# The projected queries' scratch laid out by part instead of by head

## The chip, the cores and the metric

The kernel runs on one core of a Trainium2 chip. The metric is the device time of one execution in microseconds (us); the median of several executions counts. A profile is taken of one further execution by the hardware's profiler. The engines are PE (TensorE, matrix products; PEld is its weight load), DVE (VectorE), ACT (ScalarE), POOL (GpSimd) and SP (SyncE, which here only issues transfers). Sixteen DMA engines move the data of the transfers.

## The reference

A gate mixes two branches of the same input x (2048 tokens of 512 values): attention with 32 query heads of 16 values that share one key and one value head, and a SwiGLU feed-forward of width 1792.

```python
def _A_ref(x, wq, wk, wv, wo):
    q = (x @ wq).reshape(B, S, H, Dh).transpose(0, 2, 1, 3)      # H = 32, Dh = 16
    k, v = x @ wk, x @ wv
    p = softmax(einsum("bhqd,bkd->bhqk", q, k) * Dh ** -0.5)
    o = einsum("bhqk,bkd->bhqd", p, v)
    return o.transpose(0, 2, 1, 3).reshape(B, S, H * Dh) @ wo

def _B_ref(x, w_gate, w_up, w_down):
    return (silu(x @ w_gate) * (x @ w_up)) @ w_down

g = sigmoid((x * gate_w).sum(-1, keepdims=True))
return g * _A_ref(x, ...) + (1 - g) * _B_ref(x, ...)
```

## The kernel before

**Numbers.** Everything is fp32. A product of full precision is made of three products of a faster format: each operand is split into a high part (rounded) and a low part (the rest), and high x high, high x low and low x high are added in PSUM. `load_split` (L135) does that for a weight: it loads a raw tile `wraw` (two buffers), and GpSimd writes the high part (L107) and the low part (L108).

**Queries.** `query(m, c)` (L214) projects 128 columns of the queries, which are 8 heads of 16 values, for 512 tokens: m and c each run from 0 to 3. Its `keep` leaves three parts, each 128 rows (8 heads x 16) by 512 tokens: `ql` (low), `qh` (high) and `qb`, the absolute value times the largest key, whose product with a row of -1 in the key tile is a bound that keeps the exponent safe without a maximum. `store` (L246) writes the three to a scratch in the chip's memory, `q_d`, 48 transfers of 256 KB in all. The four jobs of m = 0 run before the attention and put off their stores to `run(STORES, NCH)` (L650); the twelve others run among the first head's scores, until about 130 us. From m = 1 on, VectorE makes all three parts in buffers `hh`, `hl` (seven each) and `hs`, `ht` (two each), which are free again when their store has landed.

**Loads of a head.** `load_head(h)` (L660) brings one head's queries back. The tile `qs` (two buffers, so one head ahead) has 128 partitions: two halves of 64 rows, one for the even and one for the odd chunks of 512 tokens, and in each half the rows of high, low, high, bound. So each half needs the high part once by itself and then low, high and bound, which lie next to each other in the scratch. Head h+1 is loaded after the block in which head h starts.

**The main loop.** A unit is one head and 128 keys. `score` (L673) makes two matmuls for 1024 queries, one on each half of TensorE's rows at the same time (L680); ScalarE exponentiates (L688), on some tiles after VectorE's copy (L684); `mix` (L692) multiplies with the values (L700). The feed-forward's matmuls (L192) are put between, step by step, each job first on the lower and then on the upper half of the rows. Four units make a block. The order on each engine is written out by `block` and its tables inside `manual_schedule`; the first loads and stores before it are placed by the framework's scheduler.

**What stands in SP's queue.** Almost all transfers are issued by SP, in order: a transfer that waits for its data or its buffer holds up all behind it. Besides the stores and loads of `q_d` these are the weights (raw tiles for the first two of four passes over the feed-forward's weights, L138; the split parts are stored in the second pass, L160, and loaded in the third and fourth, L166) and a finished head's output (L714). Each transfer ends on one of eight semaphores, in turn; an instruction that needs it waits for that one.

**If the bound fails**, a plain softmax from L876 on computes everything again; with these inputs that part isn't run.

Of the kernel before, what the change touches and what calls it, by code (L numbers as in the profile page):

```python
# [8 lines left out]
F32 = mybir.dt.float32  # L9
# [9 lines left out]
P = 128  # L19
S = 2048  # L20
D = 512
H = 32
DH = 16
# [3 lines left out]
CH = 512  # L27
# [3 lines left out]
HG = P // DH  # L31
KR = 3 * DH
RT = 64
# [29 lines left out]
def tile_gated_mix(ctx, tc, x, wq, wk, wv, wo, w_gate, w_up, w_down, gate_w, out):  # L63
    nc = tc.nc
# [4 lines left out]
    dpool = ctx.enter_context(tc.tile_pool(name="dpool", bufs=1, space=DRAM))  # L69
# [1 line left out]
    ps_o = ctx.enter_context(tc.tile_pool(name="ps_o", bufs=1, space=PSUM))  # L71
    ps_f = ctx.enter_context(tc.tile_pool(name="ps_f", bufs=3, space=PSUM))

    q_d = dpool.tile([H, 3 * DH, S], F32, name="q_d")
    o_d = dpool.tile([D, S], F32, name="o_d")
    a_d = dpool.tile([NCH, P, TC, D], F32, name="a_d")
    x_d = dpool.tile([2, 2, P, KD, CH], F32, name="x_d")
# [33 lines left out]
    def three(a, b, sa, sb):  # L111
        return [(a[0][sa], b[0][sb]), (a[0][sa], b[1][sb]), (a[1][sa], b[0][sb])]
# [101 lines left out]
    def query(m, c):  # L214
        cs = slice(c * CH, (c + 1) * CH)
        t = m * NCH + c

        def terms():
            r = []
            for k in range(KD):  # L220
                r += three(WQ[m], XC[c], (slice(None), k), (slice(None), k))
            return r

        def keep(ps):
            qh = wp.tile([P, CH], F32R, name="hh", bufs=7)
            ql = wp.tile([P, CH], F32R, name="hl", bufs=7)

            if m:
                qb = wp.tile([P, CH], F32, name="ht" if c % 2 else "hs", bufs=2)
                nc.vector.tensor_copy(qh, ps)  # L230
            else:
                qb = wp.tile([P, CH], F32R, name="hl" if c % 2 else "hh", bufs=7).bitcast(F32)
                nc.scalar.activation(qh, ps, AF.Copy)
                nc.scalar.activation(qb.bitcast(F32R), ps, AF.Abs, scale=kmax)
            nc.vector.tensor_tensor(ql, ps, qh.bitcast(F32), ALU.subtract)
            if m:
                nc.vector.tensor_scalar(qb, qh.bitcast(F32), kmax, None, op0=ALU.mult)
                nc.vector.scalar_tensor_tensor(qb.bitcast(F32R), qb, -1.0, qb, op0=ALU.mult, op1=ALU.max)
            parts = [ql, qh, qb.bitcast(F32R)]
            if not m:  # L240
                for h, qs in QS.items():
                    for i, part in enumerate([qh] + parts):
                        row = c % 2 * RT + i * DH
                        nc.sync.dma_start(qs[row:row + DH, c // 2, :].bitcast(F32), part[h * DH:(h + 1) * DH].bitcast(F32))

            def store():  # L246
                for j, part in enumerate(parts):
                    nc.sync.dma_start(q_d[m * HG:(m + 1) * HG, j * DH:(j + 1) * DH, cs], part.bitcast(F32))

            if m:  # L250
                store()
            else:
                STORES.append(store)
            nc.vector.tensor_reduce(top[:, t:t + 1], qb, axis=AX.X, op=ALU.max)

        return Job(3 * KD, lambda: m in WQ, terms, keep)
# [211 lines left out]
    def output(pool):  # L468
        w = []
        for k in range(KD):  # L470
            raw = pool.tile([P, D], F32, name="os", bufs=4)
            nc.sync.dma_start(raw, wo[k * P:(k + 1) * P, :])
            w.append([pool.tile([P, D], F32R, name=f"w{x}{k}", bufs=1) for x in "hl"])
            split(w[k][0], w[k][1], raw)
        for c in range(NCH):
            o = [pool.tile([P, KD, CH], F32R, name=n, bufs=1) for n in ("oh", "ol")]
            for k in range(KD):
                raw = pool.tile([P, CH], F32, name="os", bufs=4)
                nc.sync.dma_start(raw, o_d[k * P:(k + 1) * P, c * CH:(c + 1) * CH])
                split(o[0][:, k, :], o[1][:, k, :], raw)  # L480
            for i in range(TC):
                t = c * TC + i
                ps = ps_f.tile([P, CH], F32, name="pf")
                terms = []
                for k in range(KD):
                    terms += three([x[:, k] for x in o], w[k], (slice(None), slice(i * P, (i + 1) * P)), slice(None))
                mm(ps, terms)
                at = pool.tile([P, D], F32, name="at")
                nc.sync.dma_start(at, a_d[c, :, i, :])
                ot = pool.tile([P, D], F32, name="ot")  # L490
                nc.vector.scalar_tensor_tensor(ot, ps, g_sb[:, t:t + 1], at, op0=ALU.mult, op1=ALU.add)
                nc.sync.dma_start(out[t * P:(t + 1) * P, :], ot)
# [4 lines left out]
    def new_qs(h):  # L497
        QS[h] = qsp.tile([P, 2, CH], F32R, name="qs")
        return QS[h]
# [157 lines left out]
    with tc.tile_pool(name="bpool", bufs=2) as bp:  # L657
        PT = {}

        def load_head(h):  # L660
            qs = new_qs(h).bitcast(F32)
            qv = q_d[h].rearrange("r (j b s) -> b r j s", b=2, s=CH)
            for b in range(2):

                nc.sync.dma_start(qs[b * RT:b * RT + DH], qv[b, DH:2 * DH])
                nc.sync.dma_start(qs[b * RT + DH:(b + 1) * RT], qv[b])


        def new_pt(u):
# [61 lines left out]
        def block(k, first, last, steps, kinds, order):  # L731
# [51 lines left out]
            halves.clock += 2 * LONG  # L783

        load_head(1)
        for n in range(2):
            load_w("g", n)
# [3 lines left out]
        with tc.manual_schedule():  # L791
# [25 lines left out]
            for k in range(2 * BEGIN // BLOCK, NB):  # L817
# [8 lines left out]
                h = u // NT  # L826
# [49 lines left out]
    with tc.If(rv != 0):  # L876
        with tc.tile_pool(name="gpool", bufs=2) as gp:
            with tc.For_i(0, H, 1) as h:
                qg = gp.tile([KR, S], F32R, name="qg", bufs=1)
                nc.sync.dma_start(qg[0:DH, :].bitcast(F32), q_d[bass.ds(h, 1), DH:2 * DH, :])  # L880
                nc.sync.dma_start(qg[DH:, :].bitcast(F32), q_d[bass.ds(h, 1), 0:2 * DH, :])
                for qt in range(NT):
                    pr = gp.tile([P, S], F32, name="pr")
                    mx = gp.tile([P, 3], F32, name="mx")
                    halves = []
                    for half in range(2):
                        ps = ps_s.tile([P, 2 * CH], F32, name="pss")
                        for j in range(2):
                            c = half * 2 + j
                            nc.tensor.matmul(ps[:, j * CH:(j + 1) * CH], qg[:, qt * P:(qt + 1) * P],  # L890
                                             ks[:KR, c * CH:(c + 1) * CH], start=True, stop=True)
                        nc.vector.tensor_reduce(mx[:, half:half + 1], ps, axis=AX.X, op=ALU.max)
                        halves.append(ps)
                    nc.vector.tensor_tensor(mx[:, 2:3], mx[:, 0:1], mx[:, 1:2], ALU.max)
                    nc.vector.tensor_scalar(mx[:, 2:3], mx[:, 2:3], -SCALE, None, op0=ALU.mult)
                    for half in range(2):
                        nc.scalar.activation(pr[:, half * 2 * CH:(half + 1) * 2 * CH], halves[half], AF.Exp,
                                             scale=SCALE, bias=mx[:, 2:3])
                    po = ps_o.tile([P, CH], F32, name="po")
                    for b in range(NT // TC):  # L900
                        pt = ps_f.tile([P, CH], F32, name="pf")
                        for i in range(TC):
                            kt = b * TC + i
                            nc.tensor.transpose(pt[:, i * P:(i + 1) * P], pr[:, kt * P:(kt + 1) * P], ident)
                        ptc = gp.tile([P, CH], F32, name="ptc")
                        nc.vector.tensor_copy(ptc, pt)
                        for i in range(TC):
                            kt = b * TC + i
                            nc.tensor.matmul(po[:2 * DH, :P], vaug[:, kt, :], ptc[:, i * P:(i + 1) * P],
                                             start=(kt == 0), stop=(kt == NT - 1))  # L910
                    og = gp.tile([2 * DH, 2, P], F32, name="og")
                    nc.vector.tensor_copy(og[:, 0, :], po[:2 * DH, :P])
                    nc.vector.stream_shuffle(og[:, 1, :], og[:, 0, :], [DH] * 2 * DH)
                    nc.vector.reciprocal(og[:, 1, :], og[:, 1, :])
                    nc.vector.tensor_tensor(og[:, 0, :], og[:, 0, :], og[:, 1, :], ALU.mult)
                    nc.sync.dma_start(o_d[bass.ds(h * DH, DH), qt * P:(qt + 1) * P], og[:DH, 0, :])
        with tc.tile_pool(name="upool", bufs=2) as up:
            output(up)
# [31 lines left out]
```

## Time and profile before

| what | us |
|---|---|
| median of 3 executions (1341.17 to 1343.2) | 1342.19 |
| the profiled execution, its whole time | 1340.92 |
| its span, first to last instruction | 1339.1 |
| TensorE busy | 1327.4 (99%) |
| ScalarE busy | 1069.0 (80%) |
| VectorE busy | 710.3 (53%) |
| GpSimd busy | 220.3 (16%) |
| sixteen DMA engines, transfers issued by SP | 36.4% of their span |

The busy shares are averages. The "chain" of the profile follows the last instruction back to whatever released each step; a wait on it is time that the whole kernel took longer. The rows of SP are issues: they tell when and for how long SP was occupied with a transfer, not how long the data moved. The stores of the queries run from 44 to 130 us, the loads of the heads from 71 to 1198 us.

### The profile page before, as it was taken

Reading aid. Unit: us, or ns where it says so; the run is one execution under the profiler, and the core shown is the slowest. Engines: PE = TensorE matmul, PEld = TensorE weight load, DVE = VectorE, ACT = ScalarE, POOL = GpSimd, SP = SyncE. Lnnn points to the kernel's source line nnn. Section 1 sums busy time; section 2 is a strip of 40 time slices with the busy share of each in tenths; the row PEclk is TensorE's granted clock in tenths of the full one; section 3 lists DMA queues with packets and bytes.
Section 4 is the critical chain, followed back from the end, with each engine's and each line's share of the span. In section 5 each row is a group of like instructions: output and inputs, shape, how many; then the busy total and the mean of one; then the engine's idle time right before and its main releaser. Section 6 shows DMA issues by size and latency. Waiting matters only on the chain.

```text
span 1339.1 us, 26770 instructions
## 1 busy us (share of the span) xinstructions
PE 1327.4 (99%) x10743; PEld 769.7 (57%) x10743; DVE 710.3 (53%) x1221; ACT 1069.0 (80%) x1475; POOL 220.3 (16%) x228
## 2 busy tenths in 40 slices
PE   9999999999999999999999999999999999999998
PEld 7655555555555555555555555555555555555586
DVE  4555565465455555555555555455445565455442
ACT  4578888888888888888888888888888888888511
POOL 5141321152042141143020000000000000001223
PEclk9999999999999999999999999999999999999999
DMA  8455221131135372275162342243132342333154
GB/s 278 137 178 191 67 60 36 36 105 46 54 106 156 117 232 68 68 212 159 38 206 85 127 131 84 68 133 97 52 99 68 126 147 68 99 108 115 53 184 144
DMA packets 104178, 151.84 MB, mean 113 GB/s; under 512 B 12657, under 2 KB 43633, under 8 KB 102385
## 3 DMA queue, kind: packets, MB, share of 16 engines
q1 hardware_dynamic: 102320, 149.86, 36.4%
q8 instruction: 88, 1.44, 0.5%
q10 hardware_dynamic: 1728, 0.20, 0.1%
q14 instruction: 42, 0.34, 0.1%
HBM read 98.11 MB, written 51.38 MB: 112 GB/s over the span
## 4 chain that ended last, share of the span: by engine, by line
PE 98%; DVE 1%; ACT 1%; issue 0%; POOL 0%; DVEq 0%; ACTq 0%
PE pf L192 38%; PE po L700 34%; PE pss L680 21%; PE pf L117 4%; ACT pt L688 0%; PE pss L562 0%; PE po L549 0%; DVE xl L567 0%; PE pss L602 0%; DVE acc L345 0%; DVE hs L282 0%; POOL wul L108 0%; DVE wkv_l L108 0%; ACT xh L566 0%; DVE ot L464 0%
## 5 line engine op out<-in xcount | busy, mean ns | idle before, releaser
L688 ACT ACTIVATE pt<-pss 128x1024 f32<-128x1024 f32 (+1 forms) x1024 | 842.0, 876 | 177.7 <-PE pss L680 146.5
L684 DVE COPY pt<-pss 128x512 f32<-128x512 f32 x354 | 244.8, 691 | 421.4 <-PE pss L680 386.5
L700 PE MATMUL po<-pt,vaug 128*32 128x512 f32 x4096 | 467.6, 595 | 0.0
L680 PE MATMUL pss<-qs,ks 64*128 64x512 f32 x2048 | 402.4, 417 | 1.2 <-ACT pt L688 1.1
L680 PEld LDWEIGHTS pss<-qs,ks 64*128 64x128 f32 x2048 | 193.1, 184 | 218.7 <-ACT pt L688 183.5
L700 PEld LDWEIGHTS po<-pt,vaug 128*32 128x32 f32 x4096 | 119.2, 109 | 260.3 <-issue 255.2
L688 ACT ACTIVATE pt<-pt 128x512 f32<-128x512 f32 x354 | 195.7, 620 | 0.0
L192 PE MATMUL pf<-xh,wgl 64*128 64x512 f32 (+1 forms) x440 | 162.0, 391 | 0.0
L192 PE MATMUL pf<-xh,wgh 64*128 64x512 f32 (+1 forms) x440 | 160.8, 392 | 0.3
L192 PE MATMUL pf<-xl,wgh 64*128 64x512 f32 (+1 forms) x440 | 160.3, 390 | 0.0
L192 PE MATMUL pf<-xh,wuh 64*128 64x512 f32 (+1 forms) x440 | 158.3, 392 | 1.0 <-POOL wuh L107 0.5
L192 PE MATMUL pf<-xl,wuh 64*128 64x512 f32 (+1 forms) x440 | 158.1, 390 | 0.0
L192 PE MATMUL pf<-xh,wul 64*128 64x512 f32 (+1 forms) x440 | 157.1, 391 | 0.4 <-POOL wul L108 0.4
L192 PE MATMUL pf<-wdh,hl 64*128 64x512 f32 (+1 forms) x427 | 143.8, 390 | 0.0
L192 PE MATMUL pf<-wdh,hh 64*128 64x512 f32 (+1 forms) x427 | 143.3, 390 | 0.0
L192 PE MATMUL pf<-wdl,hh 64*128 64x512 f32 (+1 forms) x427 | 143.3, 390 | 0.0
L709 DVE RECIPROCAL rsb<-rsb 128x128 f32<-128x128 f32 x128 | 117.0, 935 | 10.1 <-issue 7.8
L447 POOL CAST xh<-wraw 128x512 fp32r<-128x512 f32 x4 | 2.9, 729 | 536.8 <-DMA wraw<-o_d 536.8
L192 PEld LDWEIGHTS pf<-xh,wgh 64*128 64x128 f32 (+1 forms) x440 | 78.5, 185 | 9.6 <-issue 1.3
L192 PEld LDWEIGHTS pf<-xh,wuh 64*128 64x128 f32 (+1 forms) x440 | 77.2, 185 | 9.7 <-issue 1.9
L192 PEld LDWEIGHTS pf<-xl,wgh 64*128 64x128 f32 (+1 forms) x440 | 78.5, 185 | 5.8
L192 PEld LDWEIGHTS pf<-xh,wgl 64*128 64x128 f32 (+1 forms) x440 | 78.5, 185 | 5.4
(158 smaller groups left out, 1361.5 us busy)
## 6 DMA issues: line engine op xcount, KB each, us to landing
qs<-q_d SPq DMA_DIRECT2D x62, 192.0 KB
wraw<-in_B_w_gate_dram SPq DMA_DIRECT2D x28, 256.0 KB
wraw<-in_B_w_up_dram SPq DMA_DIRECT2D x28, 256.0 KB
wraw<-in_B_w_down_dram SPq DMA_DIRECT2D x28, 256.0 KB
wgh<-w_d SPq DMA_DIRECT2D x28, 256.0 KB
wgl<-w_d SPq DMA_DIRECT2D x28, 256.0 KB
wuh<-w_d SPq DMA_DIRECT2D x28, 256.0 KB
wul<-w_d SPq DMA_DIRECT2D x28, 256.0 KB
```

What stands on the lines that cost most here:

```text
L117: nc.tensor.matmul(ps, a, b, start=(i == 0), stop=(i == n - 1))
L192: ins = nc.tensor.matmul(self.ps, a, b, start=(i == 0 and not half), stop=(last and half != 0))
L447: nc.gpsimd.tensor_copy(OT[c][0][:, k, :], raw)
L680: nc.tensor.matmul(ps[:, b * CH:(b + 1) * CH], ks[rows, kt * P:(kt + 1) * P], QS[h][rows, j, :], start=True, stop=True)
L684: other = nc.vector.tensor_copy(pt[:, CH:], ps[:, CH:]) if half else None
L688: ins = nc.scalar.activation(pt[:, w], ps[:, w], AF.Exp, scale=SCALE)
L700: nc.tensor.matmul(po[c * 2 * DH:(c + 1) * 2 * DH, :], vaug[:, kt, :], pt[:, c * CH:(c + 1) * CH], start=(kt == 0), stop=(kt == NT - 1))
L709: nc.vector.reciprocal(rsb[:, w], rsb[:, w])
```

## The change

The scratch gets the part as its outermost dimension and the 512 rows of all heads beneath it. A store is then 128 rows on both sides. The three rows groups that a head's load took in one transfer no longer lie next to each other, so each half takes four transfers of 16 rows. The plain softmax reads its queries in three transfers.

```diff
-    q_d = dpool.tile([H, 3 * DH, S], F32, name="q_d")
+    q_d = dpool.tile([3, D, S], F32, name="q_d")
...
             def store():
                 for j, part in enumerate(parts):
-                    nc.sync.dma_start(q_d[m * HG:(m + 1) * HG, j * DH:(j + 1) * DH, cs], part.bitcast(F32))
+                    nc.sync.dma_start(q_d[j, m * P:(m + 1) * P, cs], part.bitcast(F32))
...
         def load_head(h):
             qs = new_qs(h).bitcast(F32)
-            qv = q_d[h].rearrange("r (j b s) -> b r j s", b=2, s=CH)
+            qv = q_d[:, h * DH:(h + 1) * DH, :].rearrange("i r (j b s) -> b i r j s", b=2, s=CH)
             for b in range(2):
-
-                nc.sync.dma_start(qs[b * RT:b * RT + DH], qv[b, DH:2 * DH])
-                nc.sync.dma_start(qs[b * RT + DH:(b + 1) * RT], qv[b])
+                for i, part in enumerate((1, 0, 1, 2)):
+                    row = b * RT + i * DH
+                    nc.sync.dma_start(qs[row:row + DH], qv[b, part])
...
-                nc.sync.dma_start(qg[0:DH, :].bitcast(F32), q_d[bass.ds(h, 1), DH:2 * DH, :])
-                nc.sync.dma_start(qg[DH:, :].bitcast(F32), q_d[bass.ds(h, 1), 0:2 * DH, :])
+                for i, part in enumerate((1, 0, 1)):
+                    nc.sync.dma_start(qg[i * DH:(i + 1) * DH, :].bitcast(F32), q_d[part, bass.ds(h * DH, DH), :])
```

The computing engines keep their instructions and their order. SP's queue changes. This is the place of head 15's load in it, among the weights of the second pass; before:

```order
L160 DMA w_d<-wdh 128x512
L160 DMA w_d<-wdl 128x512
L665 DMA qs<-q_d 16x2x512
L666 DMA qs<-q_d 48x2x512
L665 DMA qs<-q_d 16x2x512
L666 DMA qs<-q_d 48x2x512
L138 DMA wraw<-in_B_w_gate_dram 128x4x128
L160 DMA w_d<-wuh 128x512
L160 DMA w_d<-wul 128x512
L138 DMA wraw<-in_B_w_up_dram 128x4x128
```

And the same place with the change (L666 is now the line of all the loads, x8 counts them):

```order
L160 DMA w_d<-wdh 128x512
L160 DMA w_d<-wdl 128x512
L666 DMA qs<-q_d 16x2x512 x8
L138 DMA wraw<-in_B_w_gate_dram 128x4x128
L160 DMA w_d<-wuh 128x512
L160 DMA w_d<-wul 128x512
L138 DMA wraw<-in_B_w_up_dram 128x4x128
```

The gate weights that follow the head's load stand behind eight transfers and not four; nothing else at this place has moved.

TensorE's matmuls stay, but those that first use a head's tile wait for more transfers. Here is the start of head 3, with what each row waits for (the names are semaphores: DMAHW and a number one of the eight of SP's transfers, then those of the engines):

```order
 L192 MATMUL pf<-xh,wuh 128x512 [waits DVE_49,Pool_49]
 L192 MATMUL pf<-xl,wuh 128x512
-L680 MATMUL pss<-qs,ks 128x512 [waits DMAHW4_49,DMAHW5_49,DVE_49,Activation_49]
-L680 MATMUL pss<-qs,ks 128x512 [waits DMAHW7_49,DMAHW6_49]
+L680 MATMUL pss<-qs,ks 128x512 [waits DMAHW5_49,DMAHW6_49,DMAHW4_49,DMAHW7_49,DVE_49,Activation_49]
+L680 MATMUL pss<-qs,ks 128x512 [waits DMAHW2_49,DMAHW3_49,DMAHW1_49,DMAHW0_49]
 L192 MATMUL pf<-xl,wuh 128x512
 L192 MATMUL pf<-xh,wul 128x512
```

The first matmul, on the lower rows, waits for four transfers and two engines; the second, on the upper rows, for four transfers.

## The prediction

> **What bounds the kernel now.** I read the page's busy shares and its chain of waits first, then who waited for whom, and then only the stretches in which the queries' scratch is written or read.
>
> ```profile
> PE 1327.4 (99%) x10743; PEld 769.7 (57%) x10743; DVE 710.3 (53%) x1221; ACT 1069.0 (80%) x1475; POOL 220.3 (16%) x228
> ```
>
> TensorE is busy for 1327.4 of the span's 1339.1 us, and the chain runs through it nearly everywhere. Everything else can only cost or win time by making TensorE wait, and the waits that it has now are few. The first list below is TensorE's, of the attention and feed-forward part; the second is VectorE's from 40 to 135 us, those that name a store of the scratch.
>
> ```profile
> PE pss L680 <- ACT pt L688: 1.1, 2, 0.9
> PE pf L192 <- POOL wuh L107: 0.5, 1, 0.5
> PE pf L192 <- POOL wul L108: 0.4, 1, 0.4
> ```
>
> ```profile
> DVE hh L230 <- DMA q_d<-hh: 3.6, 1, 3.6
> DVE sign L419 <- DMA q_d<-hs: 1.6, 1, 1.6
> DVE ht L237 <- DMA q_d<-ht: 0.3, 1, 0.3
> ```
>
> No wait of TensorE names a transfer into or out of the scratch. VectorE did wait 3.6 + 1.6 + 0.3 = 5.5 us for stores, but by the windows over two stretches with many of the 48 stores (columns: window, its length, then busy time and count of PE, PEld, DVE, ACT, POOL, the clock, the DMA share, GB/s) nothing of it reached TensorE:
>
> ```profile
> 44.00:75.00 31.00, 31.00 (x225) 18.20 (x223) 15.08 (x28) 20.89 (x22) 1.91 (x2) 1.00 0.54 189
> 102.00:113.00 11.00, 11.00 (x96) 5.68 (x96) 6.51 (x11) 8.84 (x11) 2.28 (x3) 1.00 0.52 184
> ```
>
> PE is busy for the whole of each window, at the full clock; the three waits lie between 46 and 109 us. So a faster store has no wait on the path to remove, and the change can hardly make this kernel faster; the question is what its additions cost.
>
> **The stores.** Same bytes, same 48 transfers, other shape. In the windows above the DMA share sits at 0.52 to 0.54 with 184 to 189 GB/s while stores are queued without a pause: half of the sixteen engines. The nearest row for a transfer with 128 rows on both sides is a reload of stored weights late in the run (1096 to 1104 us, 40 slices):
>
> ```profile
> GB/s 0 0 0 0 0 0 0 0 0 0 0 102 41 113 256 399 379 389 399 348 144 20 113 20 20 0 0 0 0 0 123 113 41 307 410 389 359 389 410 82
> ```
>
> There 360 to 410 GB/s move. A store of 262144 B should take about 262144 / 390e3 = 0.67 us in place of 262144 / 187e3 = 1.40. The Trainium skill, "DMA: Bandwidth & Descriptors", section "Why a DMA increments its semaphore by 16 and not by 1", says that a transfer uses the largest number of engines, at most 16, that divides the outermost dimension of both sides. The trace agrees as far as the halves go: 8 outermost rows in the scratch gave about half the rate. The queue profits too. Issue times on SP (min/median/max ns; then one weight store with 128 rows on both sides, start and us):
>
> ```profile
> L248 SPq DMA_DIRECT2D q_d<-hl x18: 609/1152/1575, 44.2 to 128.4; - x18
> L665 SPq DMA_DIRECT2D qs<-q_d x62: 563/587/1216, 71.1 to 1197.1; - x62
> L666 SPq DMA_DIRECT2D qs<-q_d x62: 567/590/1257, 72.4 to 1198.1; - x62
> ```
>
> ```profile
> 574.55 0.34 SPq L160 DMA_DIRECT2D w_d<-wgh  x1
> ```
>
> A store should cost SP some 0.34 us, or 0.7 when it is backed up, for 1.15: at least 48 x 0.4 = 19 us of SP time before 130 us. What hides it is TensorE's 31.00 of 31.00 busy; its worth is 0 us. If that cover were gone, the 5.5 us of VectorE would be the most it could return.
>
> **The loads, on the transfer side.** Each head's four loads become eight. An issue costs the same for 64 KB (587 ns) as for 192 KB (590 ns), so a head's load takes SP 8 x 0.63 = 5.1 us in place of 2.5: 2.5 us more, 31 times, all of it queue time. Two places can feel it. First the head itself. The last load of head 2, on SP, and its first score, on PE:
>
> ```profile
> 117.67 0.59 SPq L666 DMA_DIRECT2D qs<-q_d  x1
> ```
>
> ```profile
> 126.06 0.40 PE L680 MATMUL pss<-qs,ks 64*128 64x512 f32 x2
> ```
>
> From that issue to the use there are 8.4 us, the least that any head has; issue to use of the transfers below is 3.2 to 5.2. The 2.5 us fit in, and before head 2 the shorter stores give them back. Worth 0.
>
> Second, what is queued behind a head's load on SP: mostly weights that stand ready for many microseconds before their use. Two are not so early, the up weights behind head 12 (485.61) and the gate weights behind head 15 (600.11), both split on GpSimd; the third row below is a load with no head's load ahead of it. SP:
>
> ```profile
> 483.08 0.57 SPq L665 DMA_DIRECT2D qs<-q_d  x1
> ...
> 485.61 0.59 SPq L138 DMA_DIRECT2D wraw<-in_B_w_up_dram  x1
> ...
> 595.39 0.39 SPq L138 DMA_DIRECT2D wraw<-in_B_w_up_dram  x1
> ...
> 600.11 0.59 SPq L138 DMA_DIRECT2D wraw<-in_B_w_gate_dram  x1
> ```
>
> GpSimd's splits, and TensorE's first use of each low part (counted in the order of instructions):
>
> ```profile
> 489.52 0.83 POOL L107 CAST wuh<-wraw 128x512 fp32r<-128x512 f32 x1 [3.74 <-DMA wraw<-in_B_w_up_dram]
> 490.43 1.28 POOL L108 TENSOR_TENSOR wul<-wraw,wuh 128x512 fp32r<-128x512 f32 x1
> ...
> 598.60 0.61 POOL L107 CAST wuh<-wraw 128x512 fp32r<-128x512 f32 x1 [1.46 <-PE pss L680]
> ...
> 605.28 0.61 POOL L107 CAST wgh<-wraw 128x512 fp32r<-128x512 f32 x1 [4.71 <-DMA wraw<-in_B_w_gate_dram]
> 605.97 1.29 POOL L108 TENSOR_TENSOR wgl<-wraw,wgh 128x512 fp32r<-128x512 f32 x1
> ```
>
> ```profile
> 493.12 0.39 PE L192 MATMUL pf<-xh,wul 64*128 64x512 f32 x1
> ...
> 608.69 0.39 PE L192 MATMUL pf<-xh,wgl 64*128 64x512 f32 x1
> ```
>
> The up weights are ready at 490.43 + 1.28 = 491.71 and used at 493.12: 1.41 us of slack. The gate weights: 605.97 + 1.29 = 607.26 against 608.69: 1.43. The whole 2.5 would leave waits of 1.1 and 1.1. But both transfers were slow because 512 KB of queries had been queued just ahead of them: issue to split took 489.52 - 485.61 = 3.91 and 605.28 - 600.11 = 5.17, where a load without that took 598.60 - 595.39 = 3.21. Spread over 5 us the queries leave the engines free sooner, so the arrival slips by 2.5 - 0.70 = 1.8 and 2.5 - 1.96 = 0.5: a wait of 0.4 for the first and none for the second. What a wait costs shows at 599 us, where TensorE waited 0.5 + 0.4 for that third load. The starts of that block's mixing and the next one's, in the chain:
>
> ```profile
> 591.44 3.57 PE po L700 x32
> ...
> 602.28 3.57 PE po L700 x32
> ```
>
> From one to the next are 10.84 us; an undisturbed block takes 1042.81 - 1033.36 = 9.45 by the last fence of this part. So 1.4 us were lost for 0.9 of waiting, some 1.6 for 1. I take 0.4 x 1.6 = **0.7 us**, with 0 and (1.1 + 1.1) x 1.6 = 3.5 as ends.
>
> **The loads, on TensorE's side.** A head's first two matmuls now wait for four transfers each and not two. Waits past the first go into instructions of their own on TensorE's queue:
>
> ```profile
> L680 PEldq EVENT_SEMAPHORE  x414: 51/51/764, 44.4 to 1251.6; - x138
> ```
>
> In the order of instructions 347 matmuls of that line have two waits, 2 three, 30 four, one five and one six; two waits to an instruction give 347 + 2 + 60 + 2 + 3 = 414, as counted. In the change it is 319, 2, 33, 4 and 24: 319 + 2 + 66 + 8 + 72 = 467. 53 more of 51 ns are 2.7 us, if none hides; 0 if all run ahead of the matmuls. The nearest row is the head's switch itself, which already has two such instructions more than other scores: the same place of two successive blocks in the chain, with the switch to head 26 and without one.
>
> ```profile
> 1033.36 0.34 PE pss L680 x2
> ...
> 1042.81 0.31 PE pss L680 x2
> ```
>
> 0.03 us for two of them; the change adds about two per switch, so 31 x 0.03 = 0.93. I take **1.0 us**.
>
> **Sum.** 0 + 0 + 0.7 + 1.0 = +1.7 us on the profiled execution's 1340.92, that is 1342.6. The median of the runs lies 1342.19 - 1340.92 = 1.3 above that execution, so 1343.9 as a median. A median of three here spans 2 us, and 0.2% (2.7 us) is about what a measurement of this kernel can tell from no change: the boundaries are 1339.5 and 1344.9.
>
> **Rivals.** *Slower, by the queue:* the head's longer load pushes the weights behind it by the full 2.5 us. It decides from 1.41 us of slip on. 3.5 us for the two places with the 1.0 of the wait instructions: 1342.2 + 4.5 = 1346.7; with all 2.7 of these, 1348.4. For it: both places are real, and each split needs another 2 us on GpSimd after the arrival. Against: the backlog that the spreading removes, 0.7 and 2.0 us of it. The skill's same page, section "Rules for kernel authors", speaks for more than that: transfers under 64 KB pay mostly overhead and should be merged. The trace disagrees for the issue, where 64 KB cost what 192 KB cost. Chance 0.32.
>
> *Faster, by the stores:* VectorE's 5.5 us of waits for stores had in truth held TensorE, and go: 1342.2 - 5.5 + 1.7 = 1338.4. For it: VectorE drains the projections' PSUM there. Against: PE's full windows. Chance 0.07.
>
> *No faster stores:* the new shape stays at half the engines, or the scratch in memory limits it. The loads come out as in the forecast, and the time too, 1343.9, since the stores were worth 0. Against it stands the reload's 390 GB/s. Chance 0.05.
>
> **How the numbers follow.** The forecast, +1.7 with stores at full width, has 0.56. Its own range is 0 to 2.7 for the wait instructions and 0 to 1 for the weights with a spread of 1 us in the median, 1341.2 to 1346. Reaching into the queue's rival, 1340.9 to 1347.0 leaves out the largest losses (about 0.1) and most of the gain (about 0.07). Faster by over 0.2%: the stores' rival, 0.07. Slower by over 0.2%: the queue's rival without its small end, 0.27, and 0.06 from the forecast's upper end, 0.33. The rest, 0.60, is within 0.2%.
>
> **What would show it.** Right: in the stretches of stores a DMA share well below 0.5 on average or 360 GB/s in bursts, and VectorE's waits for stores gone; SP's issue near 0.34 us per store and 5 us per head's load; L680's wait instructions at 467; near 493 us a wait of L192 for GpSimd's wul of under 1 us, none near 608. Wrong: a TensorE wait that names qs; blocks at a head's switch longer by more than 0.1 us; waits for GpSimd at other places; a shorter stretch from 48 to 130 us, which would mean that the stores had been on the path.

## The result, and the profile after

| | before | after |
|---|---|---|
| median, us (12 executions each, in turn) | 1342.03 (1340.49 to 1343.2) | 1345.91 (1345.55 to 1348.18) |
| the profiled execution, us | 1340.92 | 1345.91 |
| its span, us | 1339.1 | 1344.1 |

The changed kernel takes 1.0033 times as long (95% interval 1.0024 to 1.0041): 3.9 us more by the medians, 5.0 us by the two profiled executions, of which that of before lies 1.1 us under its median. It is slower by more than the 0.2% that a measurement here can tell. The time, 1345.91 us, lies inside the predicted range, but the likeliest case of the prediction, "within 0.2%" with a chance of 0.60, did not come; "slower by over 0.2%" did, which had 0.33.

The page of the changed kernel, busy time of each engine:

```profile
PE 1330.9 (99%) x10743; PEld 771.8 (57%) x10743; DVE 712.1 (53%) x1221; ACT 1069.2 (80%) x1475; POOL 220.9 (16%) x228
```

TensorE still sets the time, with the same 10743 matmuls. What it waited for, after (us in total, times, longest):

```profile
PE pf L192 <- POOL wuh L107: 1.6, 1, 1.6
PE pss L680 <- ACT pt L688: 1.1, 2, 1.0
...
PE pf L192 <- POOL wul L108: 0.6, 2, 0.4
```

One wait for the high part of up weights is new (1.6 us, at 490 us; the 0.5 of before, at 599 us, is gone); none names `qs`. That is far too little for 5 us. Where the rest is shows only in the lengths of the blocks. In TensorE's timeline the 32 mixing matmuls (L700) of a block make one row; from one such row to the next is a block. At the switch to head 26, before and after:

```profile
1026.49 3.64 PE L700 MATMUL po<-pt,vaug 128*32 128x512 f32 x32
1035.94 3.64 PE L700 MATMUL po<-pt,vaug 128*32 128x512 f32 x32
```

```profile
1030.80 3.64 PE L700 MATMUL po<-pt,vaug 128*32 128x512 f32 x32
1040.37 3.64 PE L700 MATMUL po<-pt,vaug 128*32 128x512 f32 x32
1049.77 3.64 PE L700 MATMUL po<-pt,vaug 128*32 128x512 f32 x32
```

The block with the switch took 9.45 us before and 9.57 now; the one behind it takes 9.40. I made the same differences for all blocks, from the first to the last such row, and added them by kind:

| after minus before, us | |
|---|---|
| 29 blocks with a switch (median 9.458, now 9.565) | +2.92 |
| the block that starts at 487.1 us of before (490 below) | +2.20 |
| the block that starts at 591.4 (the old wait at 599 us is shorter) | -0.39 |
| the first head, to 130 us | +0.04 |
| all others, and what lies behind the last row | +0.22 |
| sum | +4.99 |

The chain that ended last shows the same at one switch (the first row below; the second is the same place a block later): the score on TensorE stands there with 0.46 us, where it had 0.34 before.

```profile
1037.67 0.46 PE pss L680 x2
...
1047.24 0.29 PE pss L680 x2
```

What stands in that place are wait instructions of TensorE's queue, counted in the rows of L680 (x, then min/median/max ns); below them the stores and the loads on SP:

```profile
L680 PEldq EVENT_SEMAPHORE  x467: 51/51/762, 44.4 to 1256.5; - x156
```

```profile
L248 SPq DMA_DIRECT2D q_d<-hl x18: 332/452/1172, 44.2 to 122.4; - x18
...
L666 SPq DMA_DIRECT2D qs<-q_d x248: 557/590/1742, 62.1 to 1205.1; - x124
```

467 of them, 53 more, as counted beforehand. By the same view a block with a switch holds seven, where it held five before; a block without one holds three in both. 2.92 us over 53 is 55 ns for each: about all of the 51 ns that one lasts.

The one stall, at 490 us. SP, then GpSimd, then TensorE of the changed kernel:

```profile
460.11 0.32 SPq L353 DMA_DIRECT2D a_d<-acc  x1
...
485.90 5.01 SPq L666 DMA_DIRECT2D qs<-q_d  x8
490.95 0.58 SPq L138 DMA_DIRECT2D wraw<-in_B_w_up_dram  x1
```

```profile
494.32 0.61 POOL L107 CAST wuh<-wraw 128x512 fp32r<-128x512 f32 x1 [6.94 <-PE pf L192]
495.01 1.29 POOL L108 TENSOR_TENSOR wul<-wraw,wuh 128x512 fp32r<-128x512 f32 x1
```

```profile
494.99 0.50 PE L192 MATMUL pf<-xh,wuh 64*128 64x512 f32 x1 [1.58 <-POOL wuh L107]
```

The up weights behind head 12's load are issued at 490.95, not at 485.61, and their high part comes 1.58 us too late. (GpSimd's row names TensorE as what released it, but the matmuls in question had long been done; this profile has the landing too, 3.3 us after the issue, which is just before the split starts at 494.32 - 490.95 = 3.37 us.)

The stores did become faster. The two stretches that the prediction shows of before, now:

```profile
44.00:75.00 31.00, 31.00 (x225) 18.18 (x223) 15.08 (x28) 20.85 (x22) 5.09 (x6) 1.00 0.89 250
...
102.00:113.00 11.00, 11.00 (x96) 5.66 (x96) 5.68 (x10) 8.82 (x11) 0.00 (x0) 1.00 0.56 135
```

In the first the DMA share went from 0.54 to 0.89 and the rate from 189 to 250 GB/s: the stores were earlier done, and TensorE's 31.00 of 31.00 are as before. VectorE's waits for stores fell from 5.5 us to one of 2.1:

```profile
DVE hh L230 <- DMA q_d<-hh: 2.1, 1, 2.1
```

### The profile page after: what moved, and what is told of

It reads as the page before. It is cut to its first block, busy times and chain, and to the rows that moved or that the text cites. A ratio compares the mean times of both kernels' runs of the same rounds, so it can differ in the third digit from the quotient of the medians.

```text
span 1344.1 us, 26940 instructions
## 1 busy us (share of the span) xinstructions
PE 1330.9 (99%) x10743; PEld 771.8 (57%) x10743; DVE 712.1 (53%) x1221; ACT 1069.2 (80%) x1475; POOL 220.9 (16%) x228
## 2 busy tenths in 40 slices
DMA packets 106546, 151.85 MB, mean 113 GB/s; under 512 B 15024, under 2 KB 46000, under 8 KB 104752
## 4 chain that ended last, share of the span: by engine, by line
PE 96%; DMA 1%; POOL 1%; DVE 1%; ACT 1%; issue 0%; SPq 0%; DVEq 0%; POOLq 0%; ACTq 0%
PE pf L192 37%; PE po L700 34%; PE pss L680 20%; PE pf L117 4%; PE pss L562 0%; ACT pt L688 0%; DMA wraw<-in_B_w_up_dram 0%; PE po L549 0%; DMA wraw<-in_B_w_gate_dram 0%; POOL wul L108 0%; DMA wraw<-in_B_w_down_dram 0%; POOL wdl L108 0%; DVE xl L567 0%; PE pss L602 0%; DVE acc L345 0%
## 5 line engine op out<-in xcount | busy, mean ns | idle before, releaser
L700 PE MATMUL po<-pt,vaug 128*32 128x512 f32 x4096 | 467.6, 595 | 0.0
L680 PE MATMUL pss<-qs,ks 64*128 64x512 f32 x2048 | 410.0, 417 | 1.2 <-ACT pt L688 1.1
L680 PEld LDWEIGHTS pss<-qs,ks 64*128 64x128 f32 x2048 | 198.8, 184 | 218.5 <-ACT pt L688 183.1
L700 PEld LDWEIGHTS po<-pt,vaug 128*32 128x32 f32 x4096 | 119.2, 109 | 260.2 <-issue 255.3
```

The lines of the kernel that those rows point to most:

```text
L680: nc.tensor.matmul(ps[:, b * CH:(b + 1) * CH], ks[rows, kt * P:(kt + 1) * P], QS[h][rows, j, :], start=True, stop=True)
L700: nc.tensor.matmul(po[c * 2 * DH:(c + 1) * 2 * DH, :], vaug[:, kt, :], pt[:, c * CH:(c + 1) * CH], start=(kt == 0), stop=(kt == NT - 1))
```

## The experiments

Seven kernels, in two groups, each group run in turn with the kernel before on one chip (before: 1341.29 us in the first, 1341.64 in the second). Each is compared with the before of its own group (the change with that of the first table). The table tells the ratio, the wait instructions on TensorE's queue at the score line, the sum over the 29 switch blocks and their median, and the other places that moved by more than 0.5 us, by the same differences of block starts against the one profiled execution of before, whose times name the places.

| kernel | median us | ratio (95%) | wait instr. | switches, us | median | elsewhere, over 0.5 us |
|---|---|---|---|---|---|---|
| before | | 1 | 414 | 0 | 9.458 | |
| after | 1345.91 | 1.0033 (1.0024 to 1.0041) | 467 | +2.92 | 9.565 | +2.20 at 490 |
| loads_alone | 1348.04 | 1.0045 (1.0032 to 1.0058) | 467 | +3.06 | 9.567 | +2.33 at 490 |
| queue_alone | 1345.83 | 1.0034 (1.0022 to 1.0045) | 409 | +0.08 | 9.459 | +2.26 at 490, +3.5 at 128, -0.70 at 591 |
| stores_alone | 1351.58 | 1.0078 (1.0064 to 1.0091) | 414 | -0.13 | 9.458 | +6.82 at 490, +2.38 at 605 |
| four_parts | 1354.52 | 1.0100 (1.0085 to 1.0115) | 356 | -2.05 | 9.377 | +12.55 before 138, +1.59 behind it |
| after_later | 1344.50 | 1.0020 (1.0011 to 1.0030) | 474 | +2.99 | 9.566 | none over 0.5 |
| sixteen | 1369.70 | 1.0210 (1.0192 to 1.0229) | 580 | +8.14 | 9.783 | +9.22 at 490, +8.35 at 605, +0.80 at 299, -1.15 at 591 |
| again | 1339.74 | 0.9981 (0.9972 to 0.9990) | 368 | -1.70 | 9.383 | none over 0.5 |

### loads_alone: the eight transfers without the new layout

```diff
             for b in range(2):
-                nc.sync.dma_start(qs[b * RT:b * RT + DH], qv[b, DH:2 * DH])
-                nc.sync.dma_start(qs[b * RT + DH:(b + 1) * RT], qv[b])
+                for i, part in enumerate((1, 0, 1, 2)):
+                    row = b * RT + i * DH
+                    nc.sync.dma_start(qs[row:row + DH], qv[b, part * DH:(part + 1) * DH])
```

> The layout by head stays, and with it the stores on 8 rows; a head is loaded in eight transfers of 16 rows as in the changed kernel. Two theories with one answer, the wait instructions on TensorE's queue (W: 53 more on the scores' line, about 2.9 us in all at the heads' switches) and the longer stay of a head's load in SP's queue (Q: about 2 us at the up weights near 490 us): 1345 to 1347 us, 467 wait instructions on the scores' line, blocks with a head's switch about 0.1 us longer than before, one wait of TensorE for GpSimd's wuh near 490 us. The rival, that the new layout of the stores costs the time (S): 1342 us, as before.

TensorE's waits and its wait instructions:

```profile
PE pf L192 <- POOL wuh L107: 1.7, 1, 1.7
```

```profile
L680 PEldq EVENT_SEMAPHORE  x467: 51/51/755, 44.3 to 1257.2; - x156
```

With the stores as they had been, both losses are there in full (3.06 and 2.33 us), and the stretch to 130 us differs by -0.01. So the eight transfers of a head bring the whole loss without the new layout, and in the stretch of the stores the faster ones are worth nothing. The median lies 1.0 us above what was expected, and the ratio 0.0012 above the change's, which their intervals do not tell apart.

### queue_alone: the longer load without the waits

```diff
+        spare = hp.tile([RT, 2, CH // 2], F32, name="spare", bufs=1)
...
                 nc.sync.dma_start(qs[b * RT:b * RT + DH], qv[b, DH:2 * DH])
                 nc.sync.dma_start(qs[b * RT + DH:(b + 1) * RT], qv[b])
+                for i in range(2):
+                    n = (b * 2 + i) * DH
+                    nc.sync.dma_start(spare[n:n + DH], qv[b, DH:2 * DH, :, 0:CH // 2])
```

> The kernel before, with four more transfers of 16 rows (32 KB each) per head, into a spare tile that nothing reads: SP and the transfer engines get the eight issues, TensorE waits for four as before. Q alone decides: if W and Q both hold, the blocks at a head's switch stay as before (within 0.02 us) and only the wait near 490 us appears, 1343 to 1345 us. If all of the loss were the queue's: 1346 us. If all were the wait instructions': 1342 us.

Four further transfers per head go into a tile that nobody reads. TensorE's waits and wait instructions:

```profile
PE pss L683 <- ACT pt L691: 3.1, 2, 3.0
PE pf L192 <- POOL wuh L107: 1.6, 1, 1.6
```

```profile
L683 PEldq EVENT_SEMAPHORE  x409: 51/51/768, 44.1 to 1256.7; - x137
```

The stall at 490 us is there (+2.26), the switches stay as before (+0.08). So the two losses have two causes. The 3.0 us are the experiment's own: at 128 us ScalarE waited 2.5 us for a store of the queries, which the added transfers stand ahead of in SP's queue. So the time came out above the 1343 to 1345 us that were expected, and that it agrees with the change's is an accident.

### stores_alone: the new layout with four transfers per head

```diff
-                for i, part in enumerate((1, 0, 1, 2)):
-                    row = b * RT + i * DH
-                    nc.sync.dma_start(qs[row:row + DH], qv[b, part])
+                nc.sync.dma_start(qs[b * RT:b * RT + DH], qv[b, 1])
+                nc.sync.dma_start(qs[b * RT + DH:(b + 1) * RT], qv[b])
```

> The layout by part with its stores of 128 rows, but a head loaded in four transfers as before (one of 16 rows and one of 3 x 16 rows for each half). W and Q: 414 wait instructions and SP as before, 1341.3 to 1342.7 us; the stores are worth nothing, PE full from 44 to 129 us. S: 1345 to 1347 us. The author's possible hope, that full-width stores help: under 1340 us. A risk: a load with 3 outermost rows may use few transfer engines and come late, which would show as a wait for weights or a later head.

TensorE's waits:

```profile
PE pf L192 <- POOL wuh L107: 5.1, 2, 4.7
...
PE pf L192 <- POOL wgh L107: 1.2, 1, 1.2
```

The switches are again those of before (-0.13, with 414 wait instructions), and the stores again give nothing (+0.01 to 130 us). But the stall at 490 us is three times that of the change, though SP needed 3 us for a head's load and not 5. From the issue of the up weights to their split (SP, then GpSimd):

```profile
488.09 0.45 SPq L138 DMA_DIRECT2D wraw<-in_B_w_up_dram  x1
```

```profile
496.78 0.61 POOL L107 CAST wuh<-wraw 128x512 fp32r<-128x512 f32 x1 [10.19 <-DMA wraw<-in_B_w_up_dram]
```

8.69 us, where the change took 3.37. The load of three parts at once has 3 as its outermost count in the scratch. How many engines it uses can be counted, if every engine that takes part writes one small completion packet. Packets of the whole execution, stores_alone and then after:

```profile
DMA packets 103755, 151.83 MB, mean 113 GB/s; under 512 B 12234, under 2 KB 43210, under 8 KB 101962
```

```profile
DMA packets 106546, 151.85 MB, mean 113 GB/s; under 512 B 15024, under 2 KB 46000, under 8 KB 104752
```

15024 - 12234 = 2790 = 31 heads x 90. After has 8 x 16 = 128 per head, so here it is 38 = 2 x 16 + 2 x 3: three engines for each of the two large loads. The Trainium skill, "DMA: Bandwidth & Descriptors", section "Why a DMA increments its semaphore by 16 and not by 1", has this rule: the largest number of engines, at most 16, that divides the outermost size on both sides. The counts agree. They fit the stores too: loads_alone, with the old stores and the eight loads of the change, has 14640 such packets, 15024 - 14640 = 384 = 48 x 8 fewer than after, so a store ran on eight engines before and runs on sixteen now. And about three engines are all that is at work in the 3 us before the up weights are split, in which TensorE does nothing:

```profile
494.00:497.00 3.00, 0.00 (x0) 0.00 (x0) 0.00 (x0) 0.00 (x0) 0.22 (x1) 0.65 0.20 68
```

A DMA share of 0.20 is 3.2 of the sixteen engines, moving 68 GB/s: the up weights wait for those three. So the four transfers of before, kept in this layout, cost more than the eight.

### four_parts: 64 rows per head, the high part stored twice

```diff
-    q_d = dpool.tile([H, 3 * DH, S], F32, name="q_d")
+    q_d = dpool.tile([H, RT, S], F32, name="q_d")
...
-                for j, part in enumerate(parts):
+                for j, part in enumerate([qh] + parts):
...
-                nc.sync.dma_start(qs[b * RT:b * RT + DH], qv[b, DH:2 * DH])
-                nc.sync.dma_start(qs[b * RT + DH:(b + 1) * RT], qv[b])
+                nc.sync.dma_start(qs[b * RT:(b + 1) * RT], qv[b])
```

> The layout by head with the high part stored twice, 64 rows per head, so that a head is loaded in two transfers of 64 rows; 16 more stores before 130 us. W: 356 wait instructions on the scores' line in place of 414, the blocks at a head's switch 0.03 to 0.06 us shorter than before, 1340.3 to 1341.2 us. Q: SP has 1.2 us less per head, no wait of TensorE for the up weights near 490 us, nothing gained there. If wait instructions cost nothing: 1342 us. If the added stores hold VectorE long enough to reach TensorE: over 1343 us with waits before 130 us.

Two transfers of 64 rows per head and 16 more stores in the old shape. TensorE's waits, wait instructions, and the stretch from 113 to 129 us (PE first, the clock third from the end):

```profile
PE pf L192 <- DVE sign L419: 4.3, 4, 3.2
PE pss L678 <- DMA qs<-q_d: 3.0, 3, 2.5
```

```profile
L678 PEldq EVENT_SEMAPHORE  x356: 51/51/882, 43.8 to 1264.4; - x178
```

```profile
113.00:129.00 16.00, 12.85 (x96) 7.39 (x94) 6.89 (x13) 9.04 (x10) 0.71 (x1) 0.89 0.53 194
```

VectorE's waits from 40 to 135 us:

```profile
DVE ht L237 <- DMA q_d<-ht: 11.8, 3, 7.5
...
DVE hs L237 <- DMA q_d<-hs: 8.7, 4, 4.4
```

Fewer wait instructions (58) make the switches shorter, by 2.05 us in all, and there is no stall at 490 us. The price is paid elsewhere: a third more stores at half rate, for which VectorE waits 11.8 + 8.7 us, so that TensorE is busy for only 12.85 of 16 us; it also waits 3.0 us for a head's own load (`qs`), the only kernel here in which it does. The stores that TensorE does not feel at 48 transfers do reach it at 64.

### after_later: the changed kernel, heads loaded one block later

```diff
-                if k % (NT // BLOCK) == 0 and 0 < h < H - 1:
+                if k % (NT // BLOCK) == 1 and 0 < h < H - 1:
                     load_head(h + 1)
```

> The changed kernel with each head's load issued one block of 512 keys later (in the block after its predecessor's key block 0, now in the one that follows it). Theory W + Q (the loss after the change is two separate things: about 0.1 us more at each switch of head, from 53 more wait instructions on TensorE's queue, and one stall of 2.2 us at 490 us, where a head's load of 5 us stands ahead of up weights that had 1.4 us to spare): moving the load leaves the switches as they are, median near 9.56 us and +2.9 us in all against the kernel before, with 474 wait instructions; the stall at 490 us is gone if the up weights there are now issued ahead of the head's load, and then the time is 1343.3 to 1344.8 us, +2 to +3 us against the kernel before. Rival (one cause: the load's length behind everything, so the switches too): both shrink together, median at the switches near 9.46 us, time within 0.2% of before. Other rival (the load only meets another batch of weights): a wait for a weight half of 1 to 3 us at another place than 490 us, time 1345 to 1347 us.

TensorE's waits for weights, SP at the place, wait instructions:

```profile
PE pf L192 <- POOL wul L108: 0.4, 1, 0.4
PE pf L192 <- POOL wuh L107: 0.2, 1, 0.2
```

```profile
485.36 0.39 SPq L138 DMA_DIRECT2D wraw<-in_B_w_up_dram  x1
...
491.18 5.72 SPq L666 DMA_DIRECT2D qs<-q_d  x8
```

```profile
L680 PEldq EVENT_SEMAPHORE  x474: 51/51/692, 44.0 to 1253.7; - x158
```

The up weights now go ahead of the load and the stall is gone; the switches keep their +2.99. The time falls to within the interval that was expected of two separate causes. What is left against before is 2.9 us by the medians, about what the switches make up.

### sixteen: the changed kernel, each load in pieces of 8 rows

```diff
-                    row = b * RT + i * DH
-                    nc.sync.dma_start(qs[row:row + DH], qv[b, part])
+                    for e in range(0, DH, DH // 2):
+                        row = b * RT + i * DH + e
+                        nc.sync.dma_start(qs[row:row + DH // 2], qv[b, part, e:e + DH // 2])
```

> The changed kernel with each 16-row transfer of a head's load split in two of 8 rows: sixteen transfers per head instead of eight, the same bytes, the same places. Wait instructions on TensorE's queue at the score line: 580, against 467 in the changed kernel and 414 before. Theory W (each added wait instruction there costs about 0.055 us at the switch, as 53 of them cost 2.92 us): the switch blocks stand 166 x 0.055 = 9 us in all above the kernel before, some 0.3 us each, their median near 9.77 us against 9.46. Rival (the switch costs more because the head's rows are written in pieces, a fixed price whatever their number): median stays near 9.56 us, +3 us in all. Apart from the switches SyncE needs some 10 us per head's load in place of 5, so stalls for weight halves near 490 us and at other places are to be expected, 5 us or more each; the whole is then 1355 to 1375 us, and the switches are read apart from them.

Wait instructions, and the switch to head 26 in TensorE's timeline with the block behind it:

```profile
L681 PEldq EVENT_SEMAPHORE  x580: 51/51/585, 44.6 to 1277.4; - x194
```

```profile
1050.98 3.64 PE L701 MATMUL po<-pt,vaug 128*32 128x512 f32 x32
1060.77 3.64 PE L701 MATMUL po<-pt,vaug 128*32 128x512 f32 x32
1070.18 3.64 PE L701 MATMUL po<-pt,vaug 128*32 128x512 f32 x32
```

9.79 us for the switch, 9.41 behind it. A fixed price for a load in pieces would have left 9.57. From 356 to 580 wait instructions the switches' sum goes from -2.05 to +8.14 us: 10.19 / 224 = 45 ns for each. By the median switch block, which holds 3, 5, 7 and 11 wait instructions in four_parts, before, after and sixteen, the line is nearly straight: 9.377, 9.458, 9.565 and 9.783 us, 0.04 for each of the first two that are added and 0.05 for each one behind them. The stalls at 490 and 605 us are the queue's, as expected: a head's load takes SP 11.44 us here.

### again: two transfers per head, the copy made inside the memory

```diff
-    q_d = dpool.tile([H, 3 * DH, S], F32, name="q_d")
+    q_d = dpool.tile([H, RT, S], F32, name="q_d")
...
-                    nc.sync.dma_start(q_d[m * HG:(m + 1) * HG, j * DH:(j + 1) * DH, cs], part.bitcast(F32))
+                    r = RT - DH if m and j == 2 else j * DH
+                    nc.sync.dma_start(q_d[m * HG:(m + 1) * HG, r:r + DH, cs], part.bitcast(F32))
...
             for b in range(2):
-                nc.sync.dma_start(qs[b * RT:b * RT + DH], qv[b, DH:2 * DH])
-                nc.sync.dma_start(qs[b * RT + DH:(b + 1) * RT], qv[b])
+                if h < HG:
+                    nc.sync.dma_start(qs[b * RT:b * RT + DH], qv[b, DH:2 * DH])
+                    nc.sync.dma_start(qs[b * RT + DH:(b + 1) * RT], qv[b, 0:KR])
+                else:
+                    nc.sync.dma_start(qs[b * RT:(b + 1) * RT], qv[b])
+
+        def again(m):
+            hs = slice(m * HG, (m + 1) * HG)
+            nc.sync.dma_start(q_d[hs, 2 * DH:KR, :], q_d[hs, DH:2 * DH, :])
...
                     load_head(h + 1)
+                    if h in (4, 5, 6):
+                        again(h - 3)
```

> An attempt at a kernel faster than both: each head has 64 rows in the scratch (low, high, high once more, bound), so that from the ninth head on its queries are loaded by two transfers of 64 rows, not four of 32 and 96. The stores keep their form and number; the second high part of heads 8 to 31 is copied inside the memory by three transfers of 1 MB, issued with the loads of the heads behind heads 4, 5 and 6. Theory W: some 50 wait instructions fewer on TensorE's queue than the 414 of before, and the switches 24 x 0.07 = 1.7 us shorter in all (their median 9.38 us, as with two transfers of 64 rows in the run that stored the high part twice); no stall at 490 us, the stretch before 130 us unchanged; the whole 1.0 to 2.0 us under the kernel before. Rival: each copy of 1 MB (2 MB moved) takes the transfer engines for some 6 to 12 us and holds up the weights issued behind it between 200 and 300 us: waits for weight halves of 2 to 6 us there, the whole 1 to 10 us above before. Rival 2: the switches do not answer, within 0.1% of before.

Wait instructions, and SP's three copies and its loads of two transfers:

```profile
L687 PEldq EVENT_SEMAPHORE  x368: 51/51/872, 44.2 to 1250.3; - x184
```

```profile
L669 SPq DMA_DIRECT2D qs<-q_d x48: 534/592/1327, 321.1 to 1195.2; - x48
...
L673 SPq DMA_DIRECT2D q_d<-q_d x3: 737/737/745, 208.8 to 293.1; - x3
```

1339.74 against 1341.64 us, 0.9981 of it with an interval that excludes 1: the only kernel of the study that beats both. The switches, 24 of them to heads loaded in two transfers, lose 1.70 us in all. Those 24 blocks hold three wait instructions, as many as any other, and all 29 are now no longer than others (median 9.383 against 9.40 us), so I expect no more to be had there. No weight half is waited for at the copies. It is a small gain, at the bound of what can be told here.

## Why the prediction was right or wrong

**What bounds the kernel: right.** TensorE all along; no wait names the scratch before or after.

**The stores, worth 0: right.** loads_alone and stores_alone show the two halves apart: without the new stores the loss is the same, with them alone the stretch to 130 us moves by 0.01 us. Three of their details were off. VectorE's waits for stores were to go, and 2.1 of 5.5 us stayed. A store was to take 0.67 us by the rate of a reload; in the stretch with most stores (48 to 60 us) the sixteen engines were fully occupied and moved 283 GB/s, 197 before (the first row is before, the second after):

```profile
48.00:60.00 12.00, 12.00 (x83) 7.12 (x85) 6.27 (x12) 9.30 (x10) 0.00 (x0) 1.00 0.53 197
48.00:60.00 12.00, 12.00 (x83) 7.12 (x85) 6.27 (x12) 9.30 (x10) 0.00 (x0) 1.00 1.08 283
```

262144 / 283e3 = 0.93 us. And so the sign to look for, "a DMA share well below 0.5", was the wrong one: while stores are queued, faster ones show as a higher share. SP's 0.34 us for a store holds as the least (332 ns), 0.45 is the median.

**The head itself, worth 0: right.** No wait for `qs`, with loads of 5.0 us on SP as predicted.

**The wait instructions, +1.0: right mechanism, mis-sized; 2.92.** Their number, 467, was as counted. Their price came from one pair of places in the chain of before, 0.34 against 0.31 us at head 26, read as 0.03 us for the two wait instructions that a switch already had. The pair shows only the part that falls on that one step of the chain, and at one head. The same trace had a better answer, though only half of the true one: over its 29 switch blocks the median is 9.458 us, other blocks take 9.40, so two instructions cost 0.06, and 53 would cost 1.6. The runs give 35 (four_parts) to 58 ns (loads_alone) each by the counts of the table, and about its whole 51 ns where instructions are added: next to nothing hides those. The upper end that I had put down for that case, 2.7, was near the value. In the prediction's words, blocks at a switch longer by more than 0.1 us would show it wrong; they are longer by 2.92 / 29 = 0.101, so that sign came, by a hair, and it speaks of this term.

**The weights behind a head's load, +0.7: right places, mis-sized; 2.20 - 0.39 = 1.8.** The wait came where it was forecast, at the first place and not at the second, but was 1.58 + 0.17 us and not 0.4. Two parts of the working held: SP was occupied for 2.5 us more, and issue to split fell from 3.91 to 3.37, 0.54 of the 0.70 allowed for the engines being free sooner. The price of a wait was nearer 1.26 for 1 (2.20 / 1.75) than 1.6. What failed is the slack of 1.41 us, taken from one execution as if it were a constant. From the store of `acc` at 460.11 to head 12's load are 25.79 us in the change; before it was

```profile
459.10 0.32 SPq L353 DMA_DIRECT2D a_d<-acc  x1
```

with the load at 483.08, so 23.98. Between the two stands a loop in which SP and GpSimd wait for each other: a raw tile has to be split before the next may be loaded, and the split parts are stored through the same queue. Of the 490.95 - 485.61 = 5.34 us by which the up weights are late, 1.01 is TensorE's own shift, 2.52 the longer load, and 1.81 this loop. In the experiments the loop took 23.9 (four_parts) to 26.0 us (after_later, where the up weights stand in the load's place); before's profiled execution is at the short end. In again it took 25.15 us and did no harm, since a load there is 1.19 us on SP; so a long loop does not need eight transfers. Why it varies by 2 us stays open.

**Rivals.** The slower one, by the queue, named the right side but only half of the cause; its "1342.2 + 4.5", with 3.5 for the weights and 1.0 for the waits, comes out 0.8 us above the measured time, with the weights taken too high and the waits too low. The faster one falls with the result and with the stretch of the stores, which did not shrink. That the layout brings no faster stores falls with 283 GB/s. One argument against the slower one was no argument: an issue that costs the same for 64 KB as for 192 KB means that each further transfer adds a whole issue to SP's queue, which speaks for merging.

**The sum.** +1.7 on the profiled execution was predicted, +5.0 came: 1.9 of the difference of 3.3 are the wait instructions and 1.1 the weights; the last 0.3 lie scattered over the blocks. The chance of 0.60 for "within 0.2%" rested on both being small.

## What to carry to other kernels

Count what a change adds to the queue of the engine that sets the time, wait instructions too, and price them at their full recorded duration unless the trace shows them hidden; a price from one pair of rows should be held against all places of the same kind, which the starts of the blocks give. Splitting a transfer may leave its bytes and its time as they were and still cost its consumer one wait for each two pieces. And a slack of one or two microseconds behind a loop of two engines need not be a constant: before spending it, see how far that loop wanders from kernel to kernel.

## What the hardware showed beside that

**A long wait of TensorE costs its clock.** In stores_alone the wait of 4.7 us cost a block 6.82. The windows around it (the clock is third from the end):

```profile
490.00:495.00 5.00, 2.75 (x24) 1.18 (x16) 1.08 (x3) 2.47 (x4) 0.00 (x0) 0.99 0.73 217
495.00:500.00 5.00, 2.56 (x12) 2.09 (x14) 0.69 (x1) 1.04 (x2) 2.95 (x4) 0.50 0.34 116
500.00:505.00 5.00, 5.00 (x38) 3.14 (x40) 3.54 (x6) 3.92 (x7) 2.71 (x3) 0.83 0.89 278
505.00:515.00 10.00, 10.00 (x92) 5.67 (x88) 4.45 (x9) 8.49 (x13) 1.90 (x2) 1.00 0.14 44
```

The granted clock falls to 0.50 and is back at 1.00 only after 505 us; in the change itself the shorter wait (1.58 us) left it at 1.00. The waits of 6.4 and 5.9 us in sixteen brought it to 0.50 as well. The Trainium skill, "TensorE: Matmul & The Clock Gate", section "What's actually happening", puts the fall to half at one idle window of about 3.4 us; the waits of 4.7 and 1.58 us lie on either side of that.

**Few outermost rows hold up others.** Behind the two loads on three engines in stores_alone a transfer took 8.7 us from issue to split in place of 3.4, though that one has 128 rows on both sides.

**A copy inside the memory was cheap.** Three copies of 1 MB, issued at 209 to 293 us between the weights, cost SP 0.74 us each, and TensorE waited for no weight there.
